# Chunk-selected attention and gated feed-forward on one core: the first half batch prepared in a hand-written order, weight loads pinned behind the first value cast

## The chip, the cores and the metric

The kernel runs on one core of one Trainium2 chip. The metric is device time in microseconds (us) of one launch; the span inside the profile is about 1.7 us shorter. The engines are named as the profile names them: PE (TensorE matmuls), PEld (TensorE weight loads), DVE (VectorE), ACT (ScalarE), POOL (GpSimd) and SP (SyncE, which here only issues transfers).

## The reference, cut to what matters

Attention over 4 batches, 8 heads, 768 positions and 64 channels. Keys lie in 24 chunks of 32; each query attends only to six of them, picked by an upper bound computed from the minimum and maximum of each chunk's keys. The result goes through a feed-forward with a sigmoid gate.

```python
k_min = np.min(k_chunks, axis=3); k_max = np.max(k_chunks, axis=3)
ub = np.sum(np.maximum(q * k_min, q * k_max), axis=-1)      # broadcast over chunks
ub = np.where(causal, ub, -1e9)
top_chunks = np.argsort(ub, axis=-1)[..., -6:]
scores = scale * np.matmul(q, k.transpose(0, 1, 3, 2))      # masked to the chunks, and causal
attn = softmax(scores); x = np.matmul(attn, v)
gate = 1 / (1 + np.exp(-(x @ w_gate)))                      # x: 3072 x 512
out = (gate * (x @ w_val)) @ w_out                          # d_ff = 1536
```

## The kernel before

The work is cut into eight units of half a batch: 0a, 0b, 1a, ... 3b. While unit u is in its attention, the same stretch of code prepares unit u+1 (regroup, transposes, bounds, picked chunks) and runs the feed-forward of unit u-1. A scheduler orders the instructions of each engine at build time from the traced order and a model of how long things take; each engine is then given its list in that fixed order. Unit 0a has nothing to hide behind: its preparation is the start of the kernel.

```python
    def cast_v(u):                                            # values to f16, on POOL
        nc.gpsimd.tensor_copy(v16s[u.b % 2][:, u.qa:u.qb, :, 0:D], u.v)

    def load_w(i, u):                                         # copy: a wait for u's values
        ...
            nc.gpsimd.tensor_copy(wg16[:, 0, lo:lo + 1], u.v[:, HB - 1, H - 1, D - 1:D])
        nc.gpsimd.dma_start(wg16[:, :, lo:hi], wgs[:, :, lo:hi])
        nc.gpsimd.dma_start(wv16[:, :, lo:hi], wvs[:, :, lo:hi])

    def score(u, h, x):                                       # one head, one PSUM bank
        ...
        nc.scalar.activation(at[:, b0:b0 + n], ps, AF.Exp, scale=scale)
        if x == 0:                                            # the causal "mask select", on POOL
            nc.gpsimd.affine_select(out=dv, in_=dv, compare_op=ALU.is_ge, fill=0.0, ...)

    # start of the kernel (cut)
    fill_kept(0, nc.vector)                # eight copies of epat into the first key buffer
    for c, t in prep_tasks(units[0], [ppr, psc]):
        t()
    load(units[1])
    load_w(0, units[0])
    fill_kept(1, nc.gpsimd)                # the same for the second key buffer
    load_w(1, units[1]); load_w(2, units[1]); ...
```

`values(u, h)` on PE needs the mask select of its head and `cast_v(u)`. `cast_v` of unit 1a needs only the transfer of v_1a and a free buffer; nothing in the program says that it comes after the selects of unit 0a.

The softmax here doesn't subtract the row's maximum and nothing guards it: scores larger than these inputs give would overflow.

## Time and profile before

| what | before | view |
|---|---|---|
| time, median | 380.5 us | three runs |
| first exp of unit 0a | 30.0 us | timeline |
| first mask select of 0a | 30.7 us | timeline |
| first value matmul of 0b | 77.6 us | timeline |
| from there to the end of the span | 301.3 us | 378.9 less 77.6 |

The page's busy view cuts the span into 40 slices of 9.5 us. Each digit is a busy share in tenths; PEclk is the recorded clock of TensorE in tenths of full speed. Kernel before:

```profile
PE   3246317799999989999999899999999899999996
POOL 6475244012204220121214221122011101111000
PEclk9999855589999999999999999999999999999999
DMA  8999999903034623102210002000010001001002
```

From the ninth slice on, PE is at 9 nearly everywhere: the rest of the kernel is bound by PE. The first eight slices are not, and there the transfers (DMA) are busy nearly throughout. The busy-by-window view gives the numbers. Its columns are the stretch, its length, busy us with instruction counts for each engine, the recorded clock, the DMA share, and GB/s. The DMA share adds up the times of all packets, some of which overlap, so it can pass 1. Kernel before:

```profile
20.00:30.00 10.00, 5.28 (x31) 2.36 (x32) 5.34 (x21) 6.09 (x16) 7.17 (x14) 1.00 1.21 241
30.00:40.00 10.00, 6.92 (x54) 4.63 (x53) 7.62 (x24) 5.96 (x15) 5.34 (x7) 1.00 1.19 221
40.00:50.00 10.00, 1.75 (x20) 1.26 (x19) 3.15 (x8) 3.79 (x11) 0.00 (x0) 0.76 1.22 196
50.00:60.00 10.00, 4.29 (x35) 2.96 (x35) 1.86 (x4) 2.70 (x6) 4.33 (x5) 0.50 1.19 275
60.00:70.00 10.00, 7.05 (x37) 2.91 (x38) 4.71 (x10) 5.70 (x14) 3.45 (x3) 0.50 0.93 229
120.00:180.00 60.00, 56.40 (x495) 36.47 (x493) 42.63 (x110) 44.85 (x105) 11.92 (x16) 1.00 0.31 80
```

PE is busy 1.75 of 10 us in 40:50 against 56.4 of 60 us in 120:180. The waits view, limited to the first 82 us, names the reason. Its columns are who waited, for whom, total us, times and the longest. Kernel before:

```profile
POOL v_139 L178 <- DMA v_1a<-in_v_dram: 13.1, 1, 13.1
PE pv_0a_540 L291 <- POOL att_0a_464 L277: 13.3, 1, 13.3
ACT att_0a_561 L274 <- POOL k_1a L110: 12.2, 1, 12.2
```

These waits are one event, which the timeline shows. Its columns are start, duration, engine, line, operation, and in brackets the idle time before it and what ended it. Kernel before:

```profile
39.41 0.52 POOL L277 TENSOR_SCALAR_AFFINE_SELECT att_0a_431<-att_0a_431 128x384 f16<-128x384 f16 x1
53.02 1.47 POOL L178 CAST v_139<-v_1a 128x1536 f16<-128x1536 f32 x1 [13.10 <-DMA v_1a<-in_v_dram]
54.44 0.52 POOL L277 TENSOR_SCALAR_AFFINE_SELECT att_0a_464<-att_0a_464 128x384 f16<-128x384 f16 x1
55.01 0.51 PE L291 MATMUL pv_0a_540<-v_134,att_0a_464 128*128 128x65 f16 x6 [13.27 <-POOL att_0a_464 L277]
```

POOL finishes a select at 39.9 us. The next entry of its list is the cast of v_1a, a unit that is needed after 110 us. Its data lands at 53.0 us. The select of att_0a_464, whose exp had ended at 40.5, stands behind it until 54.4, and PE stands behind the select until 55.0. The Trainium skill, "TensorE: Matmul & The Clock Gate" (Specifications table at its head), says that the queue of GpSimdE is strictly first in, first out; this trace agrees, with a ready select standing 13 us behind a cast that was not.

A second thing is visible at the start. DVE had the key transposes ready in PSUM at about 6 us, but its list puts half of q's regroup (which waits for q) and eight epat copies first. Timeline of DVE, kernel before:

```profile
10.52 0.42 DVE L110 COPY q_0a<-rawq_0a 128x384 f32<-128x384 f32 x1 [0.82 <-DMA rawq_0a<-in_q_dram]
11.09 2.23 DVE L152 COPY hk_131<-epat 32x768 f16<-32x768 f16 x8
13.33 1.02 DVE L189 TENSOR_REDUCE kmm_0a<-kT_0a_167 128x12 f32<-128x384 f32 x2
```

### The profile page before, as it was taken

To read this page: it belongs to the slowest core of one execution; us is meant where nothing else is said; L and a number is where in the kernel's file an instruction comes from. 1 tells how busy PE (TensorE), PEld (TensorE's weight loads), DVE (VectorE), ACT (ScalarE), POOL (GpSimd) and SP (SyncE) were. 2 spreads that over 40 slices of the span, in tenths; PEclk is the share of its full clock that TensorE was granted. 3 is DMA by queue.
4 is the path that set the end of the run, shared out by engine and by line. 5 is a ranking of instruction groups with operands and counts; after the bars stand their busy time and mean duration, and the time that the engine had idled before them with its cause. 6 is when DMAs were issued, how large, how long until landed. Compare 5 with 4: busy or idle time off the path is not lost.

```text
span 378.9 us, 7164 instructions
## 1 busy us (share of the span) xinstructions
PE 319.8 (84%) x2704; PEld 199.0 (53%) x2704; DVE 212.9 (56%) x604; ACT 243.0 (64%) x549; POOL 81.2 (21%) x119
## 2 busy tenths in 40 slices
PE   3246317799999989999999899999999899999996
PEld 2114204376556655566466545665556556665552
DVE  3866506577535874596348857675358746331340
ACT  2375507388957794779767865889577947765331
POOL 6475244012204220121214221122011101111000
PEclk9999855589999999999999999999999999999999
DMA  8999999903034623102210002000010001001002
GB/s 211 282 240 228 196 275 206 195 0 85 5 109 116 115 78 112 56 3 84 85 57 28 2 2 78 9 2 0 29 55 2 3 28 57 2 0 57 28 3 83
DMA packets 50098, 30.34 MB, mean 80 GB/s; under 512 B 26000, under 2 KB 46992, under 8 KB 50064
## 3 DMA queue, kind: packets, MB, share of 16 engines
q1 hardware_dynamic: 45312, 25.17, 25.4%
q0 software_dynamic: 4752, 4.72, 7.3%
q8 instruction: 21, 0.34, 0.4%
q14 instruction: 13, 0.11, 0.1%
HBM read 28.31 MB, written 6.29 MB: 91 GB/s over the span
## 4 chain that ended last, share of the span: by engine, by line
PE 49%; ACT 23%; SPq 10%; DVE 8%; issue 4%; DMA 4%; POOL 1%; ACTq 0%; DVEq 0%; POOLq 0%
SPq L102 7%; SPq L96 3%; DMA v_0b<-in_v_dram 2%; ACT hq_137 L214 2%; DMA rawk_1b<-in_k_dram 2%; ACT hq_132 L214 2%; PE o_3a_4830 L327 1%; PE o_3b_5113 L327 1%; PE o_2b_4279 L327 1%; PE o_0b_1813 L327 1%; PE o_1b_3051 L327 1%; PE o_3a_4775 L327 1%; PE o_1a_2474 L327 1%; PE o_2a_3712 L327 1%; PE o_0a_1236 L327 1%
## 5 line engine op out<-in xcount | busy, mean ns | idle before, releaser
L318 PEld LDWEIGHTS <-wv_154 128*128 128x128 f16 x384 | 37.3, 98 | 31.5 <-issue 7.9
L312 PEld LDWEIGHTS <-wg_153 128*128 128x128 f16 x384 | 34.7, 98 | 15.2 <-issue 2.4
L271 PEld LDWEIGHTS <-hk_131 96*128 96x128 f16 x240 | 21.2, 106 | 10.6 <-issue 5.4
L271 PEld LDWEIGHTS <-hk_136 96*128 96x128 f16 x240 | 19.2, 97 | 9.1 <-issue 2.4
L291 PE MATMUL pv_0a_540<-v_134,att_0a_464 128*128 128x65 f16 x6 | 0.5, 244 | 13.3 <-POOL att_0a_464 L277 13.3
L274 ACT ACTIVATE att_0a_561<-sc_0a_0_562 128x512 f16<-128x512 f32 x1 | 0.6, 597 | 12.2 <-POOL k_1a L110 12.2
L295 DVE RECIPROCAL rz_0a_579<-pv_0a_540 128x6 f32<-128x6 f32 x1 | 0.2, 196 | 13.6 <-PE pv_0a_540 L291 13.6
L291 PEld LDWEIGHTS <-att_0a_464 128*128 128x128 f16 x6 | 0.4, 125 | 13.7 <-POOL att_0a_464 L277 13.7
L152 POOL COPY hk_136<-epat 32x768 f16<-32x768 f16 x8 | 6.5, 848 | 0.1
L206 PE MATMUL qT_0a_224<-ident_113,q_0a 128*128 128x128 f32 x3 | 0.9, 430 | 5.4 <-DVE hk_131 L192 5.4
L185 PE MATMUL kT_0a_167<-ident_113,k_0a 128*128 128x128 f32 x3 | 0.9, 429 | 4.9 <-DVE k_0a L110 4.9
L178 POOL CAST v_139<-v_1a 128x1536 f16<-128x1536 f32 x1 | 1.5, 1466 | 13.1 <-DMA v_1a<-in_v_dram 13.1
L257 ACT COPY hq_137<-apT_0b_615 32x384 f16<-32x384 f16 x2 | 0.9, 468 | 5.1 <-PE apT_0b_615 L252 5.1
L252 PEld LDWEIGHTS <-ap_133 128*128 128x128 f16 x20 | 1.3, 103 | 4.5 <-DVE ap_133 L246 4.5
L110 ACT COPY q_0a<-rawq_0a 128x384 f32<-128x384 f32 x2 | 1.0, 512 | 3.9 <-DMA rawq_0a<-in_q_dram 3.9
L252 PEld LDWEIGHTS <-ap_138 128*128 128x128 f16 x20 | 1.6, 106 | 3.7 <-DVE ap_138 L246 3.0
L206 PEld LDWEIGHTS qT_0a_224<-ident_113,q_0a 128*128 128x128 f32 x3 | 0.5, 213 | 5.7 <-issue 5.7
L185 PEld LDWEIGHTS kT_0a_167<-ident_113,k_0a 128*128 128x128 f32 x3 | 0.5, 212 | 4.9 <-POOL v_139 L150 4.9
L206 PE MATMUL qT_0a_234<-ident_113,q_0a 128*128 128x128 f32 x3 | 0.9, 430 | 2.6 <-DVE hk_131 L192 2.6
L178 POOL CAST v_134<-v_0a 128x1536 f16<-128x1536 f32 x1 | 1.5, 1464 | 7.3 <-DMA v_0a<-in_v_dram 7.3
L110 DVE COPY q_0a<-rawq_0a 128x384 f32<-128x384 f32 x2 | 0.8, 424 | 3.7 <-DMA rawq_0a<-in_q_dram 3.7
L110 ACT COPY k_0a<-rawk_0a 128x384 f32<-128x384 f32 x2 | 1.0, 512 | 3.0 <-DMA rawk_0a<-in_k_dram 3.0
(2045 smaller groups left out, 1104.8 us busy)
## 6 DMA issues: line engine op xcount, KB each, us to landing
wv_154<-in_moe_w_val_dram POOLq DMA_DIRECT2D x3, 512.0 KB, 9.2
wg_153<-in_moe_w_gate_dram POOLq DMA_DIRECT2D x3, 512.0 KB, 10.9
wo_155<-in_moe_w_out_dram POOLq DMA_DIRECT2D x3, 512.0 KB, 19.3
rawk_0a<-in_k_dram SPq DMA_DIRECT2D x2, 384.0 KB, 3.9
rawq_0a<-in_q_dram SPq DMA_DIRECT2D x2, 384.0 KB, 7.8
v_0a<-in_v_dram SPq DMA_DIRECT2D x3, 256.0 KB, 8.7
rawk_0b<-in_k_dram SPq DMA_DIRECT2D x2, 384.0 KB, 5.0
rawq_0b<-in_q_dram SPq DMA_DIRECT2D x2, 384.0 KB, 6.0
```

Of the source, the lines that this page charges most:

```text
L96: nc.sync.dma_start(t[:, 4 * j:4 * j + 4], src[u.b, 4 * j:4 * j + 4, u.rows].rearrange("h (p x) d -> p h x d", x=HB))
L102: nc.sync.dma_start(u.v[:, i], v[u.b, :, r:r + 128].rearrange("h p d -> p h d"))
L110: f(t[:, :, h0:h1, :], raw[:, h0:h1].rearrange("p h x d -> p x h d"))
L152: eng.tensor_copy(headK[i][64:96, h, :], epat)
L178: nc.gpsimd.tensor_copy(v16s[u.b % 2][:, u.qa:u.qb, :, 0:D], u.v)
L206: nc.tensor.transpose(ps[:, x:T:HB], u.q[:, x, 2 * p:2 * p + 2, :].rearrange("p h d -> p (h d)"), ident32)
L214: nc.scalar.copy(headQ[u.half][0:64, 2 * p + e, :], ps[64 * e:64 * e + 64])
L252: nc.tensor.transpose(ps[:, 128 * x:128 * x + 128], apt[j][:, x, :, :].rearrange("p h c -> p (h c)"), ident16)
L271: nc.tensor.matmul(ps[:, o:o + w], headK[u.b % 2][:, h, 128 * jb:128 * jb + 128], headQ[u.half][:, h, i:i + w], start=True, stop=True)
L312: nc.tensor.matmul(gp, wg16[:, c, 128 * fb:128 * fb + 128], u.xT[:, c, :], start=(c == 0), stop=(c == 3))
L318: nc.tensor.matmul(vp, wv16[:, c, 128 * fb:128 * fb + 128], u.xT[:, c, :], start=(c == 0), stop=(c == 3))
L327: nc.tensor.matmul(op, hgl[(u.name, fc)][:, 128 * tb:128 * tb + 128], wo16[:, fc, :], start=(fc == 0), stop=(fc == NFB - 1))
```

## The change

The intent: prepare unit 0a sooner, by an order written by hand for every engine, and keep the weights from taking DMA time away from the first loads. The weight loads are pinned ("kept in program order") behind what was traced before them on POOL: the first pair comes behind the cast of v_0a, the rest is spread over unit 0a's attention. The core of the diff, with cuts marked:

```diff
-    fill_kept(0, nc.vector)
 ...
-    def load_w(i, u):
+    def load_w(i):
         lo, hi = 512 * i, 512 * i + 512
-        if u is not None:
-            nc.gpsimd.tensor_copy(wg16[:, 0, lo:lo + 1], u.v[:, HB - 1, H - 1, D - 1:D])
-        nc.gpsimd.dma_start(wg16[:, :, lo:hi], wgs[:, :, lo:hi])
+        tc.keep_in_program_order(nc.gpsimd.dma_start(wg16[:, :, lo:hi], wgs[:, :, lo:hi]))
 ...                                        # the same for w_val and w_out
+    def first_prep(u):
+        A, V, G = nc.scalar.copy, nc.vector.tensor_copy, nc.gpsimd.tensor_copy
+        regroup(u, "k", [(V, 0, 2), (A, 2, 4)])
+        regroup(u, "k", [(V, 4, 6), (A, 6, 8)])
+        for p in range(NP):
+            keys_t(u, p, (ppr, ppr, psc, psc)[p])
+            keys_f(u, p, SS)                # both key copies of a pair on ACT
+        regroup(u, "q", [(A, 0, 2), (G, 2, 4), (A, 4, 6), (G, 6, 8)])
+        for p in range(NP):
+            queries_t(u, p, (psc, ppr, ppr, psc)[p])
+ ...                                        # chunks, bounds and picks of head group 0 early
+        cast_v(u)
+ ...
-    for c, t in prep_tasks(units[0], [ppr, psc]):
-        t()
     load(units[1])
-    load_w(0, units[0])
-    fill_kept(1, nc.gpsimd)
 ...
+    with tc.manual_schedule():
+        fill_kept(0, nc.gpsimd)
+        first_prep(units[0])
+    load_w(0)
 ...
+        if i == 0:
+            a.append((0.0, lambda: fill_kept(1, nc.gpsimd)))
+            for n in range(3):
+                a.insert(len(a) * (n + 1) // 4, ...)          # load_w(1), load_w(2), load_wo
```

For the later units, `prep_tasks` is rewritten too: the value cast follows the chunk copies, the bounds of the two head groups are two tasks with both copies on ACT, and both picks come before both transposes of the picks.

More of the change, by code (lines that the diff above doesn't have):

```diff
@@ L77, in __init__ @@
             self.width = base
-            self.att, self.pv = {}, {}
+            self.att, self.pv, self.kps, self.qps, self.ubT = {}, {}, {}, {}, {}
     LOW = [
@@ L102, in load, with regroup @@
             nc.sync.dma_start(u.v[:, i], v[u.b, :, r:r + 128].rearrange("h p d -> p h d"))
-    def regroup(u, n):
+    def regroup(u, n, parts):
         raw = getattr(u, "raw" + n)
-        t = nat.tile([128, HB, H, D], F32, tag=n, name=f"{n}_{u.name}")
-        setattr(u, n, t)
-        def move(f, h0, h1):
+        if not hasattr(u, n):
+            setattr(u, n, nat.tile([128, HB, H, D], F32, tag=n, name=f"{n}_{u.name}"))
+        t = getattr(u, n)
+        for f, h0, h1 in parts:
             f(t[:, :, h0:h1, :], raw[:, h0:h1].rearrange("p h x d -> p x h d"))
-        if u is units[0]:
-            for j in (0, 4):
-                move(nc.vector.tensor_copy, j, j + 2)
-                move(nc.scalar.copy, j + 2, j + 4)
-        else:
-            move(nc.gpsimd.tensor_copy, 0, H)
     load(units[0])
@@ L164, with load_wo @@
     wos = moe_w_out.rearrange("(c p) f -> p c f", p=128)
-    def load_w(i, u):
+    def load_w(i):
         lo, hi = 512 * i, 512 * i + 512
-        if u is not None:
-            nc.gpsimd.tensor_copy(wg16[:, 0, lo:lo + 1], u.v[:, HB - 1, H - 1, D - 1:D])
-        nc.gpsimd.dma_start(wg16[:, :, lo:hi], wgs[:, :, lo:hi])
-        nc.gpsimd.dma_start(wv16[:, :, lo:hi], wvs[:, :, lo:hi])
-    def load_wo(i, u):
-        nc.gpsimd.tensor_copy(wo16[:, 4 * i, 0:1], u.v[:, HB - 1, H - 1, D - 1:D])
-        nc.gpsimd.dma_start(wo16[:, 4 * i:4 * i + 4, :], wos[:, 4 * i:4 * i + 4, :])
+        tc.keep_in_program_order(nc.gpsimd.dma_start(wg16[:, :, lo:hi], wgs[:, :, lo:hi]))
+        tc.keep_in_program_order(nc.gpsimd.dma_start(wv16[:, :, lo:hi], wvs[:, :, lo:hi]))
+    def load_wo(i):
+        tc.keep_in_program_order(nc.gpsimd.dma_start(wo16[:, 4 * i:4 * i + 4, :], wos[:, 4 * i:4 * i + 4, :]))
     def cast_v(u):
@@ L189, in keys_t, with keys_f @@
             nc.vector.tensor_reduce(out=u.kmm[:, p, e, :], in_=pv, op=op, axis=AX.X)
-        hk = headK[u.b % 2]
-        nc.scalar.copy(hk[0:64, 2 * p, u.rows], ps[0:64])
-        nc.vector.tensor_copy(hk[0:64, 2 * p + 1, u.rows], ps[64:128])
+        u.kps[p] = ps
+    def keys_f(u, p, engs):
+        ps = u.kps.pop(p)
+        for e in range(2):
+            engs[e](headK[u.b % 2][0:64, 2 * p + e, u.rows], ps[64 * e:64 * e + 64])
     def chunks_t(u):
@@ L212, in queries_t, with queries_f, bounds @@
             nc.vector.tensor_scalar_min(u.qs[64:128, 2 * p + e, s0:T], src[:, s0:T], 0.0)
+        u.qps[p] = ps
+    def queries_f(u, p, engs):
+        ps = u.qps.pop(p)
         for e in range(2):
-            nc.scalar.copy(headQ[u.half][0:64, 2 * p + e, :], ps[64 * e:64 * e + 64])
-    def bounds(u):
+            engs[e](headQ[u.half][0:64, 2 * p + e, :], ps[64 * e:64 * e + 64])
+    def bounds(u, j):
         s0 = 128 * u.sel0
         n = T - s0
-        u.ubT = []
-        for j in range(2):
-            ps = ppr.tile([128, T], F32, tag="ps", name=f"ubT_{u.name}_{j}")
-            for i in range(4):
-                nc.tensor.matmul(ps[32 * i:32 * i + 32, 0:n], kcat[u.b % 2][:, 4 * j + i, :],
-                                 u.qs[:, 4 * j + i, s0:T], start=True, stop=True)
-            t = ubp.tile([128, T], F32, tag="ubT", name=f"ubTs_{u.name}_{j}")
-            if j == 0:
-                nc.scalar.copy(t[:, 0:n], ps[:, 0:n])
-            else:
-                nc.vector.tensor_copy(t[:, 0:n], ps[:, 0:n])
-            u.ubT.append(t)
+        ps = ppr.tile([128, T], F32, tag="ps", name=f"ubT_{u.name}_{j}")
+        for i in range(4):
+            nc.tensor.matmul(ps[32 * i:32 * i + 32, 0:n], kcat[u.b % 2][:, 4 * j + i, :],
+                             u.qs[:, 4 * j + i, s0:T], start=True, stop=True)
+        t = ubp.tile([128, T], F32, tag="ubT", name=f"ubTs_{u.name}_{j}")
+        nc.scalar.copy(t[:, 0:n], ps[:, 0:n])
+        u.ubT[j] = t
     def pick(u, j):
@@ L336, in ffn_tasks, with prep_tasks @@
         return r + [(2.6, lambda tb=tb: ffn_out(u, tb)) for tb in range(HB)]
-    def prep_tasks(u, pools):
-        n = [0]
-        def pool():
-            n[0] += 1
-            return pools[n[0] % len(pools)]
-        r = [(0.0, lambda: regroup(u, "k")), (0.0, lambda: regroup(u, "q"))]
+    VS = (nc.vector.tensor_copy, nc.scalar.copy)
+    SV = (nc.scalar.copy, nc.vector.tensor_copy)
+    SS = (nc.scalar.copy, nc.scalar.copy)
+    GP = [(nc.gpsimd.tensor_copy, 0, H)]
+    def prep_tasks(u):
+        r = [(0.0, lambda: regroup(u, "k", GP)), (0.0, lambda: regroup(u, "q", GP))]
         for p in range(NP):
-            r.append((0.4, lambda p=p: keys_t(u, p, pool())))
-        r.append((0.0, lambda: chunks_t(u)))
+            r.append((0.4, lambda p=p: (keys_t(u, p, ppr), keys_f(u, p, SV))))
+        r.append((0.0, lambda: (chunks_t(u), cast_v(u))))
         for p in range(NP):
-            r.append((0.4, lambda p=p: queries_t(u, p, pool())))
-        r.append((0.45 * u.m, lambda: bounds(u)))
-        r.append((0.0, lambda: cast_v(u)))
+            r.append((0.4, lambda p=p: (queries_t(u, p, ppr), queries_f(u, p, SS))))
+        for j in range(2):
+            r.append((0.22 * u.m, lambda j=j: bounds(u, j)))
         for j in range(2):
             r.append((0.13 * u.m, lambda j=j: pick(u, j)))
+        for j in range(2):
             r.append((0.06 * u.m, lambda j=j: pick_t(u, j)))
         return r
+    def first_prep(u):
[8 more added lines that the diff above has]
+            queries_t(u, p, (psc, ppr, ppr, psc)[p])
+            if p == 1:
+                chunks_t(u)
+                queries_f(u, 0, SS)
+                queries_f(u, 1, SV)
+                bounds(u, 0)
+        cast_v(u)
+        pick(u, 0)
+        queries_f(u, 2, SS)
+        bounds(u, 1)
+        queries_f(u, 3, SS)
+        pick_t(u, 0)
+        pick(u, 1)
+        pick_t(u, 1)
     def merge(a, f):
@@ L394, in attend_tasks @@
         return r + prep + pending
-    for c, t in prep_tasks(units[0], [ppr, psc]):
-        t()
     load(units[1])
-    load_w(0, units[0])
-    fill_kept(1, nc.gpsimd)
-    load_w(1, units[1])
-    load_w(2, units[1])
-    for i in range(3):
-        load_wo(i, units[1])
+    with tc.manual_schedule():
+        fill_kept(0, nc.gpsimd)
+        first_prep(units[0])
+    load_w(0)
     prev = []
@@ L408 @@
         if i + 1 < len(units):
-            prep = prep_tasks(units[i + 1], [ppr])
+            prep = prep_tasks(units[i + 1])
         a = attend_tasks(u, prep)
@@ L412 @@
             a.insert(len(a) // 2, (0.0, lambda i=i: load(units[i + 2])))
+        if i == 0:
+            a.append((0.0, lambda: fill_kept(1, nc.gpsimd)))
+            for n in range(3):
+                a.insert(len(a) * (n + 1) // 4, (0.0, (lambda n=n: load_w(n + 1)) if n < 2 else (
+                    lambda: [load_wo(j) for j in range(3)])))
         merge(a, prev)
```

## The prediction

> **What bounds the kernel now.** Two regimes. From about 78 us to the end the busy-by-window view shows PE at 56 to 59 us of every 60 (93 to 99%): PE-bound, clock 1.00. The first 78 us are not: PE is busy 39 us of 80, and the DMA share stays near 1.2 (saturated) from 10 to 60 us. The chain of waits up to 82 us is 45% SP DMA issue plus 18% waiting for v_0b and rawk_1b. The visible damage: POOL's value cast for unit 1a stood ahead of unit 0a's mask selects, POOL waited 13.1 us for v_1a (39.9 to 53.0), and PE waited 13.3 us behind it (att_0a_464). The Trainium skill, "TensorE: Matmul & The Clock Gate" (specifications table), says GpSimd executes strictly in order; this trace agrees: a ready select waited 13 us behind a cast. PE then ran at clock 0.50 from 47 to 76 us. The first exp comes at 30.0 us, the first value matmul of unit 0b at 77.6.
>
> **What the change does.**
> 1. Hand order for 0a's preparation; DVE loses eight epat copies (2.2 us) and POOL gets them (8 x 0.82 us). In the timeline DVE's first kmm reduction started at 13.3 us although its transpose ended near 6; now it can start near 5.5. I chain: keys to 11, q regroup to 11.5, qs of two pairs to 15.5, bounds 17, pick 21, mask rows 23. First exp near 24 instead of 30.
> 2. Weight loads leave the first 15 us: v_0a lands about 12 instead of 14.1. Total DMA work is unchanged. The Trainium skill, "DMA: Bandwidth & Descriptors" (Queues, rings and completion order), says each engine round-robins between queues by packet; so later weights take their share from 1a and 1b instead. From the landings (0a plus one weight load by 14.1; all four units and nine weight loads by about 60.6) I estimate 10 us per unit and 2.3 per weight load.
> 3. Program order on POOL: the cast of v_1a no longer stands before 0a's selects; it and v_1b's come after the last one, before 0b's first. So the 13 us stall disappears. New costs on POOL: eight copies for the second key buffer (0.82 each) and the DMA issues (0.8 each) sit between selects; cast v_0b (landing about 23) and five copies precede the first select, so it comes about 29, not 24. The early first exp is mostly lost there.
>
> After that I replay the measured pieces: from the first value matmul (35.9) to the stall 8 us, from its end to 77.6 another 23. New: values start near 30, 0a's selects end near 40, the serial 0b preparation (queries, bounds, picks) takes about 21 us more, to 60. v_1b's cast must also precede 0b's first select: all DMA ends near 60, so 60 to 62.5. PE-bound operation starts near 62 instead of 78; the later order of instructions is almost the same (bounds' second copy moves DVE to ACT, 0.5 us a unit, hidden), so the gain passes through whole.
>
> **Predicted:** 364 us, 8 in 10 between 357 and 371. Faster by over 2%: 0.91; within 2%: 0.07; slower: 0.02.
>
> **Right or wrong shows as:** first exp near 24 us; first select near 29; no wait of POOL for v_1a over 3 us inside 0a's attention; first 0b value matmul 58 to 65; the span from there to the end about 301 us as now; PE still at clock 0.5 for part of 30 to 60.
>
> **What would make it wrong:** v_1b landing past 65 (weights starving the loads), turning the v_1a stall into a v_1b stall: about 370. Or the preparation of 0b warm and shorter, v_1b by 54: about 357. Or the PE-bound part stretching by a worse interleave, which I put at 2 us either way.

## The result, and the profile after

The changed kernel takes 368.0 us (366.0 to 369.0, four runs) beside 380.7 us. The ratio is 0.9653, 95% interval 0.9605 to 0.9701. Ratios here are the mean time of one kernel's runs over the mean of the other's from the same rounds, so not quite the ratio of the quoted medians. The busy view of the page after:

```profile
PE   3353757999999899998999899999999899999996
POOL 9729832022132221122042201112011011110000
PEclk9999955699999999999999999999999999999999
DMA  8999999920319222031210001000100010001002
```

PE's row of nines now begins a slice earlier, and the hole in its fifth and sixth slices (3 and 1 before) is mostly filled (7 and 5). The busy-by-window view of the changed kernel:

```profile
20.00:30.00 10.00, 3.70 (x23) 1.67 (x21) 4.81 (x25) 5.61 (x14) 4.66 (x5) 1.00 1.15 270
30.00:40.00 10.00, 6.59 (x61) 5.71 (x62) 4.45 (x11) 4.81 (x12) 8.92 (x14) 1.00 1.11 264
40.00:50.00 10.00, 5.64 (x52) 3.83 (x49) 7.65 (x17) 7.19 (x20) 5.40 (x8) 0.84 1.21 196
50.00:60.00 10.00, 7.57 (x39) 3.17 (x37) 4.65 (x15) 4.76 (x12) 4.34 (x3) 0.50 1.19 218
60.00:70.00 10.00, 7.90 (x53) 5.55 (x53) 4.83 (x29) 5.79 (x12) 1.04 (x2) 0.50 1.10 233
```

PE is busy 5.64 us in 40:50 instead of 1.75, but only 3.70 in 20:30, where it was 5.28 before. The waits view of the first 82 us, changed kernel:

```profile
POOL att_0b_672 L268 <- ACT att_0b_672 L265: 7.2, 1, 7.2
POOL v_134 L167 <- DMA v_0b<-in_v_dram: 5.3, 1, 5.3
PE pv_0a_354 L282 <- POOL att_0a_318 L268: 5.8, 1, 5.8
```

The wait for v_1a has gone. POOL now waits 5.3 us for v_0b and PE 5.8 us for the first select. The timeline, changed kernel:

```profile
26.53 1.47 POOL L167 CAST v_134<-v_0b 128x1536 f16<-128x1536 f32 x1 [5.27 <-DMA v_0b<-in_v_dram]
28.06 3.92 POOL L145 COPY hk_136<-epat 32x768 f16<-32x768 f16 x5
32.06 0.51 POOL L268 TENSOR_SCALAR_AFFINE_SELECT att_0a_318<-att_0a_318 128x384 f16<-128x384 f16 x1
32.63 0.51 PE L282 MATMUL pv_0a_354<-v_134,att_0a_318 128*128 128x65 f16 x6 [5.80 <-POOL att_0a_318 L268]
```

The first exp ended at 26.4 us, but the first select comes at 32.1 us, which is 1.4 us later than before the change: POOL's list has the cast of v_0b (landed at 26.4) and five epat copies for the second key buffer in front of it. The first value matmul of 0b marks the start of PE-bound operation. Timeline of PE, kernel before:

```profile
77.63 0.98 PE L291 MATMUL pv_0b_726<-v_134,att_0b_675 128*128 128x65 f16 x14
```

and the changed kernel:

```profile
68.05 1.03 PE L282 MATMUL pv_0b_723<-v_134,att_0b_672 128*128 128x65 f16 x15
```

It comes at 68.1 us instead of 77.6, and from there to the end of the span are 298.8 us instead of 301.3. So 9.6 us were won before PE-bound operation and 2.5 us in it.

### The profile page after: what moved, and what is told of

It is laid out like the page before. It is cut to its first block, busy times and chain, and to the rows that moved or that the text cites. A ratio compares the mean times of both kernels' runs of the same rounds, so it can differ in the third digit from the quotient of the medians.

```text
span 366.9 us, 7168 instructions
## 1 busy us (share of the span) xinstructions
PE 320.4 (87%) x2704; PEld 201.2 (55%) x2704; DVE 204.5 (56%) x581; ACT 247.5 (67%) x560; POOL 88.5 (24%) x125
## 3 DMA queue, kind: packets, MB, share of 16 engines
q1 hardware_dynamic: 45312, 25.17, 25.8%
## 4 chain that ended last, share of the span: by engine, by line
PE 60%; ACT 19%; DVE 8%; SPq 4%; DMA 3%; issue 3%; POOL 2%; ACTq 0%; POOLq 0%
DMA v_0b<-in_v_dram 3%; SPq L102 3%; ACT hq_137 L210 2%; ACT hq_132 L210 2%; SPq L96 1%; POOL hk_136 L145 1%; DVE hk_131 L184 1%; DVE hk_136 L184 1%; PE o_2b_4223 L318 1%; PE o_1b_2995 L318 1%; PE o_0b_1757 L318 1%; PE o_3a_4827 L318 1%; PE o_2a_3709 L318 1%; PE o_0a_1233 L318 1%; PE o_1a_2471 L318 1%
## 5 line engine op out<-in xcount | busy, mean ns | idle before, releaser
L145 POOL COPY hk_136<-epat 32x768 f16<-32x768 f16 x8 | 6.4, 822 | 0.3
L145 POOL COPY hk_131<-epat 32x768 f16<-32x768 f16 x8 | 6.4, 845 | 0.1
L198 PE MATMUL qT_0a_212<-ident_113,q_0a 128*128 128x128 f32 x3 | 0.9, 440 | 4.0 <-ACT q_0a L110 4.0
L178 DVE TENSOR_REDUCE kmm_0b<-kT_0b_342 128x12 f32<-128x384 f32 x2 | 1.1, 558 | 5.7 <-PE kT_0b_342 L174 5.7
L217 PE MATMUL ubT_0a_236<-qs_0a,kcat_130 128*32 128x256 f32 x8 | 1.6, 634 | 2.4 <-ACT kcat_130 L190 2.4
L295 PEld LDWEIGHTS <-xnat_0a 128*128 128x128 f16 x12 | 1.2, 118 | 4.2 <-issue 4.2
L217 PE MATMUL ubT_0a_277<-qs_0a,kcat_130 128*32 128x256 f32 x8 | 1.1, 631 | 2.3 <-DVE ubm_0a_263 L231 2.3
```

Of the source, the lines that this page charges most:

```text
L145: eng.tensor_copy(headK[i][64:96, h, :], epat)
L217: nc.tensor.matmul(ps[32 * i:32 * i + 32, 0:n], kcat[u.b % 2][:, 4 * j + i, :], u.qs[:, 4 * j + i, s0:T], start=True, stop=True)
```

## The experiments

The question is which part of the change made the gain, and what held the early part's share below the 16 us of the prediction (62 us instead of 78). Theory A says that the gain is the removed stall on POOL. Its rivals say that it is the earlier first preparation, or that the first 60 us are bound by the transfers, whatever POOL does. Twelve kernels were run; all gave correct results. They ran in three groups on different chips, each with the kernel before in the same rounds; across groups the ratios are the fairer comparison, and the text says where they differ from the medians.

### b_vpin: the kernel before, with only the value casts kept in order

```diff
-        nc.gpsimd.tensor_copy(v16s[u.b % 2][:, u.qa:u.qb, :, 0:D], u.v)
+        tc.keep_in_program_order(nc.gpsimd.tensor_copy(v16s[u.b % 2][:, u.qa:u.qb, :, 0:D], u.v))
```

> The kernel before with one edit: each value cast is kept behind what was traced before it on POOL, so the cast of v_1a no longer stands ahead of the mask selects of unit 0a. Theory A (the gain of the change is the removed POOL stall): POOL no longer waits 13 us inside 0a's attention, the first 0b value matmul comes near 66 us instead of 77.6, and the time is about 369 us. Rival B (the first 60 us are bound by the transfers, so a removed wait only turns into another one): first 0b value matmul after 73 us, time 375 to 381 us.

Measured: 368.3 us (367.7 to 370.7), ratio 0.9678 (0.9629 to 0.9727). The first value matmul of 0b came at 64.8 us, b_vpin:

```profile
64.79 0.98 PE L291 MATMUL pv_0b<-v,att_0b 128*128 128x65 f16 x14
```

Timeline of POOL over the old stall, b_vpin:

```profile
38.72 0.52 POOL L277 TENSOR_SCALAR_AFFINE_SELECT att_0a<-att_0a 128x384 f16<-128x384 f16 x1 [0.75 <-ACT att_0a L274]
40.74 0.52 POOL L277 TENSOR_SCALAR_AFFINE_SELECT att_0a<-att_0a 128x384 f16<-128x384 f16 x1 [1.50 <-ACT att_0a L274]
41.52 1.46 POOL L110 COPY k_1a<-rawk_1a 128x1536 f32<-128x1536 f32 x1 [0.26 <-PE kT_0b L185]
```

The selects follow each other where the 13 us hole was. One line of code gives what the whole change gives, within the intervals. Theory A stands in this sense: removing the stall is enough for a gain of this size. The transfers did not turn the removed wait into another one in this kernel, although the DMA share stayed near 1.2 until 60 us.

The line keeps the casts of all units in order, but the part after 0b's first value matmul gained nothing from that (302.1 us, 301.3 before), so the gain lies in the first stretch.

This has two limits. The equal totals are made up differently: b_vpin reaches 0b's first value matmul 3.3 us before the changed kernel and then takes 302.1 us to the end against 298.8, so the other edits of the change lose about as much as they win. And the change with the stall left in was not run, nor was it tried which of its edits moved the cast of v_1a. a_nohand has no wait for v_1a either, so the forced order is not needed for it.

### a_nohand: the changed kernel without the forced order

```diff
-    with tc.manual_schedule():
-        fill_kept(0, nc.gpsimd)
-        first_prep(units[0])
+    fill_kept(0, nc.vector)
+    first_prep(units[0])
```

> The changed kernel with the hand-written order of the first preparation dropped (the scheduler orders it; the epat copies of the first key buffer are back on DVE); the weight loads and the POOL order of the value casts stay. Theory A (the hand order is worth nothing, the POOL order is all): 366 to 369 us as the changed kernel or less, first select no later than 32 us. Rival C (the earlier first preparation carries a good part of the gain): 5 or more us slower, 373 us.

Measured: 365.2 us (364.7 to 365.5), ratio 0.9584 (0.9547 to 0.9621), so about 2.8 us faster than the changed kernel. The first exp came at 23.6 us instead of 25.8. The timeline of ACT shows one difference. The first line is from the changed kernel, where q's regroup on ACT stands behind eight key copies by order:

```profile
11.32 0.92 ACT L110 COPY q_0a<-rawq_0a 128x384 f32<-128x384 f32 x2
```

and this one from a_nohand, where the scheduler took q first:

```profile
6.69 0.51 ACT L110 COPY q_0a<-rawq_0a 128x384 f32<-128x384 f32 x1 [0.70 <-DMA rawq_0a<-in_q_dram]
```

The first query transpose ran at 7.4 us instead of 11.9. But most of that lead is gone at the first bound matmuls (15.4 us against 15.8). The larger part of the 2.2 us is lost at the pick that follows. In the changed kernel the masking of the bounds (ubm), whose input PE had ready at 20.0 us, stands in DVE's list behind the queries of the other two pairs. Timelines of PE and DVE, changed kernel:

```profile
19.38 0.63 PE L228 MATMUL ubN_0a_260<-ident_113,ubTs_0a_241 128*128 128x128 f32 x2
21.57 0.43 DVE L204 TENSOR_SCALAR qs_0a<-qT_0a_251 64x256 f32<-64x256 f32 x1 [0.45 <-ACT qs_0a L203]
22.03 0.26 DVE L231 TENSOR_TENSOR ubm_0a_263<-ubN_0a_260,pen 128x96 f32<-128x96 f32 x1
```

In a_nohand it ran at 19.1 us, as soon as its input was there. This kernel also moves the first buffer's epat copies back to DVE, so it is not yet a clean test of the order; d_hand_vpin below is. And it has a new wait, on POOL:

```profile
62.46 1.47 POOL L167 CAST v<-v_1b 128x1536 f16<-128x1536 f32 x1 [13.47 <-DMA v_1b<-in_v_dram]
```

### a_filllate: the second key buffer's copies kept behind the last select of 0a

```diff
-            a.append((0.0, lambda: fill_kept(1, nc.gpsimd)))
+            a.append((0.0, lambda: fill_kept(1, nc.gpsimd, tc.keep_in_program_order)))   # memsets and copies
```

> The changed kernel with the eight epat copies and two memsets of the second key buffer kept behind the last select of 0a on POOL. Theory D (the five copies between the cast of v_0b and the first select cost 4 us of the critical path, and two more between selects 0.8 us each): first select at 28.1 instead of 32.1 us, time 4 us less, about 364 us. Rival E (the serial preparation of 0b, which needs no select, sets the pace): first select at 28.1 but the time within 1 us of the changed kernel.

Measured: 364.3 us (363.4 to 365.1), ratio 0.9561 (0.9513 to 0.9608), 3.7 us below the changed kernel. Theory D holds: the five copies lay on the critical path. POOL's timeline, a_filllate:

```profile
27.14 1.47 POOL L167 CAST v<-v_0b 128x1536 f16<-128x1536 f32 x1 [5.18 <-DMA v_0b<-in_v_dram]
28.57 1.01 POOL L268 TENSOR_SCALAR_AFFINE_SELECT att_0a<-att_0a 128x384 f16<-128x384 f16 x2
63.01 1.47 POOL L167 CAST v<-v_1b 128x1536 f16<-128x1536 f32 x1 [10.95 <-DMA v_1b<-in_v_dram]
```

The select follows the cast directly, at 28.6 us. But the wait for v_1a has come back as a wait for v_1b: 11.0 us of POOL in front of 0b's first select, for values that are needed a batch later. In the changed kernel v_1b landed at 54.8 us, and POOL waited 0.2 us for it; here and in a_nohand it landed between 62 and 63 us. In these two, POOL reached the second pair of weight loads at 30 to 31 us, before SP began to issue the three loads of v_1b (at 34.1 and 35.5 us), and the three issues then took 21 us together. In the changed kernel the weight loads came at 35.5 us, behind two of v_1b's three issues (from 33.7 us on), and these took 5.3 us together. The Trainium skill, "DMA: Bandwidth & Descriptors" (Queues, rings and completion order), says that each engine takes turns between the queues it has work for, packet by packet. These landings fit it: what was issued while the other queue had work took longer, although it was needed first. No run moved these weight loads alone, so that they delayed v_1b is argued and not shown.

### a_w0late: the first pair of weight loads moved behind the third select

```diff
-    load_w(0)                       # behind the cast of v_0a
+    # load_w(0) joined to load_w(1), a quarter into the attention of 0a
```

> The changed kernel with the first pair of weight loads moved from 13.6 us to behind the third select of 0a, beside the second pair. Theory F (these loads take DMA time from v_0b, which gates POOL): v_0b lands near 23 instead of 26.4 us, first select near 26.5 (only two epat copies are left after the cast in this order), time about 363 us. Rival: v_0b lands as late as before (26 us), or the first gate matmuls then wait for the weights, time 367 us or more.

Measured: 367.2 us (365.6 to 367.7), ratio 0.9630 (0.9587 to 0.9672). The first half of theory F held: v_0b's cast ran at 23.0 us, without a wait, and the first select came at 26.7 us. The rival held as well. The waits view of 26 to 66 us, a_w0late:

```profile
PE v_0a L309 <- DMA wv<-in_moe_w_val_dram: 2.8, 1, 2.8
```

The gate matmuls of 0a stand in PE's list amid the attention, and the late weights kept PE waiting 2.8 us. Of the 5.2 us by which the first values came earlier (27.5 against 32.6 us), 1.9 us were left at 0b's first value matmul (66.2 us), and the time was no better than the changed kernel's, within the intervals. So neither place for the first pair of weight loads is better.

### c_nohand_vpin: a_nohand, with the value casts kept in order

The edit is that of b_vpin, on a_nohand.

> The changed kernel without the hand order (as in a_nohand), and in addition each value cast kept behind what was traced before it on POOL: v_1b's cast, for which POOL waited 13.5 us in a_nohand, then comes after 0b's selects. Theory G (in a_nohand and a_filllate the early wait came back as a wait for v_1b, worth 3 to 4 us): no POOL wait for a DMA over 1 us between 40 and 70 us, first 0b select near 57 instead of 63.9 us, time near 361.5 us. Rival (0b's start is bound by something else, as the PE's clock): 364 us or more.

Measured: 360.9 us (360.5 to 361.5), ratio 0.9480 (0.9452 to 0.9508). The first select of 0b, c_nohand_vpin:

```profile
56.32 0.52 POOL L268 TENSOR_SCALAR_AFFINE_SELECT att_0b<-att_0b 128x384 f16<-128x384 f16 x1 [8.50 <-ACT att_0b L265]
```

It waited only for its exp, and came at 56.3 instead of 63.9 us. The signs of theory G came as expected: in a_nohand the removed wait had partly come back as a wait for v_1b. But the 4.3 us below a_nohand are not v_1b's alone. The edit also moved the cast of v_0b on POOL, from 25.0 us, in front of the first select, to 30.0 us, behind the third, and 0a's first values came at 25.1 instead of 27.1 us. The two were not tried apart. In the other pair, a_filllate and c_late_vpin below, the same edit gave 1.2 us, within the intervals.

### c_late_vpin and d_hand_vpin: is the hand order worth anything?

c_late_vpin is a_filllate with the value casts of the units after the first kept in order. d_hand_vpin differs from c_nohand_vpin in the forced order alone:

```diff
-    fill_kept(0, nc.vector)
-    first_prep(units[0])
+    with tc.manual_schedule():
+        fill_kept(0, nc.vector)
+        first_prep(units[0])
```

> The changed kernel with the hand order kept, the second key buffer's copies after 0a's last select (as in a_filllate) and the value casts of all later units kept in traced order. Theory G: first select of 0a about 26.5 us (not held by v_0b any more), no wait for v_1b, time 360 to 361 us. Against c_nohand_vpin this is also the fair test of the hand order with POOL's order mended on both sides: if the hand order is worth anything it is faster than c_nohand_vpin by 1 us or more; if it is worth nothing they are within 1 us.

> c_nohand_vpin with the first preparation traced in the same order but forced, engine by engine, by the manual schedule: the cleanest test of the hand-written order itself (POOL's order is nearly the same, the epat copies of the first key buffer are on DVE in both). Theory K (the hand order costs time, because ScalarE must finish the eight key copies before it moves its half of q, so the first query transpose comes at 11.9 instead of 7.4 us): first query transpose 10 us or later, first exp 25.5 us or later against 23.6, time 1 to 3 us above c_nohand_vpin (362 to 364 us). Rival (the c_late_vpin difference came from the later key buffer copies): within 0.5 us of c_nohand_vpin.

Measured: c_late_vpin 363.1 us (360.6 to 363.9), ratio 0.9525 (0.9482 to 0.9568), 2 us above the 360 to 361 that theory G had put there; d_hand_vpin 362.9 us (361.1 to 363.4), ratio 0.9500 (0.9467 to 0.9534). With the forced order the first query transpose came at 12.4 us and the first exp at 26.3 us in d_hand_vpin, against 7.4 and 23.6 us without. The reason that theory K gave, ACT's key copies in front of q, is the smaller part: the first bound matmuls ran only 0.9 us later (16.3 against 15.4 us), but ubm on DVE 3.4 us later (22.5 against 19.1 us), behind the other pairs' queries as in the changed kernel. In all three pairs (a_nohand, c_late_vpin, d_hand_vpin) the forced order was slower by 2 to 3 us in the median. In the last pair, the cleanest, each ratio lies within the other's interval, and by the ratios the difference is 0.8 us. So the statement that is safe is that the order written by hand gains nothing here; that it costs 1 to 2 us is likely and not shown. What is useful in it is the choice of engines (half of q on POOL, none on DVE), which the unforced kernels keep.

### b_vpin_q: b_vpin, with DVE's half of q's regroup moved to POOL

```diff
-                move(nc.vector.tensor_copy, j, j + 2)
+                move(nc.vector.tensor_copy if n == "k" else nc.gpsimd.tensor_copy, j, j + 2)
```

> b_vpin with the DVE half of unit 0a's q regroup moved to POOL, nothing else: DVE then no longer waits for q in front of the key reductions. Theory L (the early weight loads' POOL instructions, which wait for v_0b and end near 30.4 us, gate the first select, so an earlier first preparation is worth nothing while they stand there): first exp 3 to 5 us earlier (near 26 us), first select still near 30.6 us, time within 2 us of b_vpin's 368.3. Rival M (the earlier preparation helps by itself): time 364 us or less.

Measured: 366.0 us (365.7 to 366.5), ratio 0.9591 (0.9563 to 0.9619), 2.3 us below b_vpin (3.3 by the ratios). Neither theory got it whole. The first exp came 3.6 us earlier (26.4 us) and the first select at 30.5 us all the same, as theory L said: POOL's list has the weight copies that wait for v_0b and five DMA issues in front of it. But two heads were then ready at once and the first values started 3.6 us earlier (32.2 us), of which 2.3 to 3.3 us reached the end.

### c_pff, c_warm, d_warmctl, d_pff_warm: the serial preparation of 0b

With POOL's order mended, what is left before PE-bound operation is the chain of 0b's queries, bounds and picks, some 26 us (34.8 to 60.7 us in c_nohand_vpin). c_pff gives its query transposes two of the PSUM buffers that the feed-forward does not use yet:

```diff
-            ... queries_t(u, p, ppr) ...
+            ... queries_t(u, p, pff if u is units[1] and p % 2 else ppr) ...
```

> c_nohand_vpin with the query transposes of unit 0b spread over the two preparation buffers and two of the idle feed-forward PSUM buffers. Theory H (the serial 0b preparation is held by two PSUM buffers: each query pair waits for the copies of the pair two before, 2.3 us a pair): the four pairs take about 6 instead of 9.5 us, time 2 to 3 us under c_nohand_vpin. Rival I (ScalarE's own work, four copies or relus a pair, sets 2 us a pair): within 1 us of it.

Measured: 357.4 us (356.1 to 358.3), ratio 0.9385 (0.9352 to 0.9417), 3.5 us below c_nohand_vpin. The last query transpose ended at 41.4 instead of 46.3 us. The timeline of PE, c_pff, shows how:

```profile
20.59 1.12 PE L198 MATMUL qT_0b<-ident,q_0b 128*128 128x128 f32 x4
22.64 0.69 PE L198 MATMUL qT_0b<-ident,q_0b 128*128 128x128 f32 x2
```

Two of the four pairs now ran before 0a's first exp (24.5 us), where c_nohand_vpin ran its first pair at 34.8 us; the other two ran at 35.7 and 40.9 us. So theory H is right that the two buffers held the chain, but not in its picture of four pairs in 6 us: the scheduler used the free buffers to start early. The last pair took 0.49 us instead of 0.90, so a part of the gain may be the clock's.

c_warm puts four needless 128x512 matmuls after each of ten pieces of that chain; d_warmctl the same with two columns:

```diff
+    def warm(n=4):
+        ps = pff.tile([128, 512], F32, tag="ff", name=f"warm{len(warmed)}")
+        for _ in range(n):
+            tc.keep_in_program_order(nc.tensor.matmul(ps, ident16, wsrc, start=True, stop=True))
 ...                                        # d_warmctl: ps[:, 0:2] and wsrc[:, 0:2]
```

> c_nohand_vpin with groups of four needless 128x512 f16 matmuls into an idle PSUM buffer after each piece of 0b's query preparation, to keep TensorE busy. Theory J (the granted clock of 0.5 between 45 and 65 us stretches the chain by its PE pieces): clock 1.0 in 40 to 65 us, the bound matmuls 0.8 instead of 1.5 us, time 2 to 4 us under c_nohand_vpin. Rival: the clock falls all the same, or the added matmuls cost what they save: no gain or slower.

> c_warm with the needless matmuls cut to two columns, so that they fix the same instruction order points but keep TensorE hardly busy: control for c_warm. Theory J (c_warm's 3 us come from the clock): clock back at 0.5 somewhere in 40 to 60 us and the time 1.5 us or more above c_warm's 357.8. Rival N (they come from the changed PE order): within 1 us of c_warm, whatever the clock.

Measured: c_warm 357.8 us (357.7 to 358.0), ratio 0.9399 (0.9369 to 0.9429); d_warmctl 360.8 us (359.7 to 362.3), ratio 0.9456 (0.9422 to 0.9489). The first bound matmuls (the same eight) in the timeline of PE, c_warm:

```profile
45.08 0.85 PE L219 MATMUL ubT_0b<-qs_0b,kcat 128*32 128x384 f32 x8
```

and d_warmctl:

```profile
46.53 0.87 PE L219 MATMUL ubT_0b<-qs_0b,kcat 128*32 128x384 f32 x4
```

The eight take 0.85 us in the one and 1.51 us in the other, so the control ran at about half the speed of c_warm. These and the three later query transposes (0.90 us each against 0.52 to 0.55) make up 1.7 us. The times agree with theory J: the low clock of a little-used PE costs the chain 3.0 us by the medians, 2.2 us by the ratios, whose intervals just touch. The control is not quite clean: its traced order differs, about 50 of PE's 2704 other matmuls stand elsewhere in the list, so rival N is not excluded for a part of this. The expected sign, a clock of 0.5 somewhere in 40 to 60 us, came from 55 us on. Before that the record misleads: in d_warmctl it reads 1.00 in 40 to 50 us, where the durations say half. The record of the windows, d_warmctl:

```profile
40.00:50.00 10.00, 6.39 (x54) 3.25 (x52) 5.16 (x11) 6.46 (x16) 3.44 (x4) 1.00 1.18 231
50.00:60.00 10.00, 7.31 (x57) 4.51 (x55) 5.20 (x32) 4.84 (x10) 0.52 (x1) 0.74 1.11 226
```

The Trainium skill, "TensorE: Matmul & The Clock Gate" (Part 1, Seeing it yourself), warns that these clock events have been seen to be unreliable on trn2; this case agrees, and the durations decide.

d_pff_warm joins both:

> Both mendings of the 0b preparation at once: the query transposes over two more PSUM buffers and the needless matmuls. If the two gains are apart (3.5 and 3.0 us under c_nohand_vpin) the time is about 354.5 us; if the shorter chain leaves less for the clock to stretch, 355 to 357 us. The transfers, saturated until about 60 us, are the rival bound: then the first 0b value matmul stays above 57 us.

Measured: 356.5 us (355.8 to 357.1), ratio 0.9336 (0.9309 to 0.9363), the fastest of all. It is 0.9 us below c_pff by the medians, 1.9 by the ratios, and their intervals overlap. Below c_nohand_vpin it is 4.4 us (5.5 by the ratios), where the two gains apart add up to 6.5: they overlap in part. Whether that is because a shorter chain leaves less for the clock to stretch, or because of the transfers, stays open: 0b's first value matmul came at 56.8 us, just under the 57 us that the rival asked for. c_pff is the version to keep, because it has no needless work: 357.4 us, against 368.0 for the change and 381 for the kernel before.

| kernel | median us | ratio to before |
|---|---|---|
| changed kernel | 368.0 | 0.9653 |
| b_vpin (one line on the kernel before) | 368.3 | 0.9678 |
| b_vpin_q | 366.0 | 0.9591 |
| a_w0late | 367.2 | 0.9630 |
| a_nohand | 365.2 | 0.9584 |
| a_filllate | 364.3 | 0.9561 |
| c_late_vpin | 363.1 | 0.9525 |
| d_hand_vpin | 362.9 | 0.9500 |
| c_nohand_vpin | 360.9 | 0.9480 |
| d_warmctl | 360.8 | 0.9456 |
| c_warm | 357.8 | 0.9399 |
| c_pff | 357.4 | 0.9385 |
| d_pff_warm | 356.5 | 0.9336 |

## Why the prediction was right, point by point

- *The gain is the removed POOL stall.* Right: b_vpin mends nothing but the order of the casts and takes 368.3 us beside the change's 368.0. No wait of POOL for v_1a is left in the changed kernel, as forecast. That the change's other edits cancel so nearly is chance.
- *Time 364 us, 357 to 371.* 368.0 us lies inside, 4 us above the centre.
- *First exp near 24 us.* 25.8 us. The steps up to the bounds came within 1 us of the text (their copy ended at 18.0 us, where it said 17). The pick ended at 23.3 us instead of 21: the text missed that DVE's list has the queries of the other two pairs, until 22.0 us, in front of it.
- *v_0b lands about 23, first select about 29.* This term was mis-sized: v_0b landed at 26.4 and the select came at 32.1 us, so 0a's first values came at 32.6 instead of 30. The mechanism (first weight loads, cast and five copies in front of the select) was right. a_w0late has it landed by 23.0 when the two weight loads go, and a_filllate puts 3.7 us of the total on the second buffer's copies.
- *Serial preparation of 0b, 21 us, to about 60.* It took 25.1 us, from the first query transpose of 0b at 43.0 to the first value matmul at 68.1. Counted as the prediction counted, from the last select of 0a, it took 23.5 us, and that select ended at 44.5 instead of 40. The 21 us had been read off a stretch in which one of the four query pairs was already done. c_pff and c_warm show, on c_nohand_vpin, what can be taken out of the chain: 3.5 us with more PSUM buffers and 2 to 3 us with a busier PE, not all of it together.
- *v_1b's landing as a second bound, 60 to 62.5 us.* Wrong for the changed kernel: v_1b landed at 54.8 and POOL then waited 7.2 us for an exp. But the wait is real and near: a_nohand and a_filllate ran into it, at 62 to 63 us.
- *First value matmul of 0b between 58 and 65.* Missed: 68.1 us. The terms of the prediction add up to 61: values from 30, ten more to the last select, 21 for the chain. They measured 2.6, 1.9 and 2.5 us more. (One replayed figure was misread too: from the first value matmul to PE's stall are 5.9 us before the change, 35.9 to 41.7, not 8.)
- *The rest about 301 us, as before.* It was 298.8. (The trace of the kernel before has PE busy 56 to 57 us of every 60 here, not up to 59.) All kernels with the change's `prep_tasks` that did not wait inside it for v_1b, without or with needless matmuls, have 297.6 to 298.8 us from the first value matmul of 0b to the end of the span; the before-like ones (b_vpin, b_vpin_q) have 301.5 to 302.1. So some part of the reordered later preparation is worth about 2.5 us. Which part was not tried apart, and stays open. The prediction had this part right only as a size. The 2.5 us made up for some of what was lost before it. Without them the time would have been near 370.5 us, at the upper end of the range; that it lies well inside is luck.

## What to carry to other kernels

On an engine that runs its list strictly in order, an instruction that waits for a transfer blocks everything behind it (13 us here); look at what a scheduler put in front of the first instruction that PE is waiting for, and pin work whose input may still be on its way and whose result is needed late (a cast of the next batch's values) behind it before writing any order by hand. After each such repair read the trace again, because the same wait may come back one tile later. In this kernel the start-up phase of short dependent pieces was also paid in the low clock of a little-used PE (2 to 3 us) and in PSUM buffers that stood unused until the main phase (3.5 us). An order forced by hand can put a ready step behind others just as a scheduler can, as ubm did here.

## What the Trainium skill lacked or had wrong

- "TensorE: Matmul & The Clock Gate" warns that recorded clock events can be unreliable, but not how that looks: here the record reads 1.00 until the first event that it holds (at about 38.5 us in the kernel before). The kernel before reads 1.00 in 30:40, while its three 128x128 f32 transposes at 31.8 us took 0.87 us together, as in the stretch recorded at 0.50 (0.88 us at 57.2 us); at 40.2 us the same took 0.53 us. Matmul durations are the safer reading.
- The same page advises to keep PE busy, but gives no figure for doing so with needless matmuls: forty of them won 2 to 3 us here against a control with the same instructions on two columns (357.8 and 360.8 us, ratios 0.9399 and 0.9456).
- No page that was read says what an instruction whose input comes late and whose result is not yet needed costs on an in-order engine: 13.1 us of POOL for a 1.5 us cast in the kernel before, and 13.5 and 11.0 us for v_1b in a_nohand and a_filllate.
- "DMA: Bandwidth & Descriptors" does not tell how a loaded queue looks at the issuing engine: in the kernel before, SP's issue of one 256 KB load took 0.5 us for the first (v_0a, at 2.9 us), 3.4 us for the next, and up to 7.6 us later (v_1a, from 24.0 us on).
